# Loading each half batch of x by sixteen transfers of 112 tokens

## The chip, the cores and the metric

The program runs on one core of a Trainium2 chip. The core has a matrix engine (TensorE, PE in the profile), a vector engine (VectorE, DVE), a scalar engine (ScalarE, ACT), GpSimd (POOL) and SyncE (SP), each with an instruction queue of its own that it works off in order, and 16 DMA engines, which move data between the chip's memory and the on-chip buffer. In this kernel SyncE and ScalarE issue plain transfers and GpSimd issues the indexed ones. The metric is the device time of one execution, in microseconds (us); less is better.

## The reference

Two layers are computed one after the other. The first is a causal convolution over time with a softmax over its seven taps, with one set of taps for each of eight heads of 24 channels:

```python
x_pad = np.concatenate([np.zeros((B, pad, D), dtype=np.float32), x], axis=1)
x_unf = x_pad[:, idx, :].reshape(B, S, K, H, group)
out = np.einsum('hk,bskhg->bshg', w, x_unf)      # B, S, D = 8, 3584, 192; K = 7; H = 8
```

The second is a mixture of eight experts over the 28672 tokens that come out. Tokens and experts are paired greedily by their logits, with room for 3584 tokens in each expert, and every token then goes through the two layers of its expert:

```python
logits = x @ w_gate
...                                               # each token to one expert, 3584 per expert
h = np.maximum(x[mask] @ w1[e], 0.0)              # D = 192 -> F = 1024
out[mask] = h @ w2[e]                             # F -> D
```

## The kernel before

The tokens are cut into 16 half batches of 1792 tokens, and a half batch into 16 runs of W = 112 tokens. The convolution is a matrix product: the tile `X` of a half batch has 118 partitions (six tokens of halo and 112 of the run), 16 runs and 192 channels, and `TH[0:118, h]` is the banded matrix of head h. `conv(i)` runs the eight heads: a matmul into one of four PSUM banks named `cv`, which ScalarE copies into the tile `a`. Behind the eighth copy ScalarE issues the store of `a` into the table `attn` in memory (L209). There are two buffers `a`, so the first copy of conv(i) has to wait until the store of half batch i-2 has landed.

`load(i)` fills X by two transfers from SyncE: the halo (L194 where a batch begins, with a memset by GpSimd beside it, otherwise L197) and the 112 tokens of all 16 runs (L198). There are three X buffers. The main loop over i issues load(i+2), then conv(i), whose store follows, so a half batch adds a halo, a load and a store to the transfers, in that order in the program. load(i+2) takes the buffer of conv(i-1), and SyncE waits for the matmuls of that.

Between the heads of conv(i), the function `mid` gives out the work of the half batches before: transposes `aT` on VectorE, the split of `aT` into `hi` (ScalarE) and `lo` (GpSimd, sometimes VectorE), and the matmuls `pl` of the gate's logits for half batch i-2. The hooks add steps of the routing (threshold, counts, lists; tiles such as `X0`, `X1`, which the profile also names X, and `oa`, `bg`, `t_t`), mostly on VectorE. In which order they are given out is set when the program is built, by a model of the three compute engines' pace that leaves DMAs out of account. At i = 14 SyncE is given the first six transfers of expert weights (`raw`, L1142 to L1145), behind load 15. After the 16 half batches the experts run: gathers of rows of `attn` (GpSimd), matmuls `ph` and `y`, and indexed stores of the result.

Every transfer of SyncE and ScalarE signals its landing on one of eight semaphores. The program takes these in turn over the transfers of both engines, in the program's order, and a transfer that takes a semaphore again is issued only after the transfer eight before it, the last one on that semaphore, has landed.

Of the kernel before, what the change touches and what calls it, by code (L numbers as in the profile page):

```python
# [14 lines left out]
NE, D, NTOK, F, CAP = 8, 192, 28672, 1024, 3584  # L15
W, HW_, NHB = 112, 16, 16
# [95 lines left out]
def build(ctx, tc, nc, x, weight, wg, attn, LT, wk):  # L112
# [75 lines left out]
    def load(i):  # L188
        t = X[i] = k.xp[i % 3].tile([118, 16, D], F32, name="X")
        b, hf = divmod(i, 2)  # L190
        o = x.offset + (b * 3584 + hf * 1792) * D
        if hf == 0:
            P.memset(t[0:6, 0], 0.0)
            nc.sync.dma_start(t[0:6, 1:16], bass.AP(tensor=x.tensor, offset=o + (W - 6) * D,  # L194
                                                    ap=[[D, 6], [W * D, 15], [1, D]]))
        else:
            nc.sync.dma_start(t[0:6], bass.AP(tensor=x.tensor, offset=o - 6 * D, ap=[[D, 6], [W * D, 16], [1, D]]))  # L197
        nc.sync.dma_start(t[6:118], bass.AP(tensor=x.tensor, offset=o, ap=[[D, W], [W * D, 16], [1, D]]))  # L198

    def conv(i, mid):  # L200
        t = X.pop(i)
# [58 lines left out]
    def logits_t(i):  # L260
# [10 lines left out]
        if not last:  # L271
            V.tensor_tensor(o, o, v[:, 1], op=OP.add)

    k.load, k.conv, k.transp, k.split, k.logits, k.logits_t = load, conv, transp, split, logits, logits_t
    k.toeplitz, k.gate_ops, k.transp_last, k.logits_last = toeplitz, gate_ops, transp_last, logits_last
    return k
# [1336 lines left out]
```

## Time and profile before

| | |
|---|---|
| time, median of 3 runs | 1388.71 us (1386.31 to 1390.99) |
| the profiled execution, its time | 1390.04 us |
| its span, first to last instruction | 1388.2 us |
| mean granted TensorE clock | 0.971 of full speed |
| TensorE busy | 1303.3 us (94%) |
| VectorE busy | 1074.7 us (77%) |
| ScalarE busy | 631.2 us (45%) |
| GpSimd busy | 737.2 us (53%) |
| SyncE's DMA queue (q1) | 63888 packets, 120.75 MB |
| ScalarE's DMA queue (q10) | 28928 packets, 22.02 MB |
| loads of x (L198) | 16 transfers of 1344 KB |
| stores of `attn` (L209) | 16 transfers of 1344 KB |

The profile is of one execution. Engines are busy side by side, so the busy times add up to more than the span. Most calls of VectorE, ScalarE and TensorE pass through one helper, so their rows all bear line 53 and are told apart by their tiles. A row of the timeline has start, duration, engine, line and operation, `out<-in` by the tiles' names, and in brackets how long the engine sat idle just before and what released it. A DMA's row shows how long its issue took, not when it landed; when a transfer landed is seen where an engine waits for it, and from the rows of the DMA queues, which give packets, MB and the time that the packets took as a share of the 16 engines in a window.

### The profile page before, as it was taken

How to read it: one execution, taken by the hardware profiler on the slowest of the kernel's cores; microseconds unless marked ns; L12 is line 12 of the kernel's file. 1: busy time of each engine (PE TensorE's matmuls, PEld its weight loads, DVE VectorE, ACT ScalarE, POOL GpSimd, SP SyncE). 2: the span in 40 equal slices, each digit the busy share in tenths (PEclk: the TensorE clock that was granted, in tenths of full speed). 3: DMA queues.
4: the chain of work that ended last, by engine and by line, in shares of the span. 5: the costliest groups of instructions: out<-in, count | busy, mean ns of one | idle time of the engine just before them, and what ended most of it. 6: DMA issues, size and time to landing. Idle time of an engine off the chain costs nothing.

```text
span 1388.2 us, 21399 instructions
## 1 busy us (share of the span) xinstructions
PE 1303.3 (94%) x7459; PEld 1110.2 (80%) x7459; DVE 1074.7 (77%) x2358; ACT 631.2 (45%) x1292; POOL 737.2 (53%) x729
## 2 busy tenths in 40 slices
PE   5988898998989999999999999999999999999997
PEld 2544565887878888888888888888888888888886
DVE  7598963876988988888765778788787888878782
ACT  4745474567645555454334333333333333333331
POOL 5655466668866766666554444444443444444322
PEclk9988897999989999999999999999999999999999
DMA  9996668659771432432232251324322213141100
GB/s 230 287 263 164 171 214 283 225 193 299 261 242 54 141 134 93 139 132 84 94 122 75 96 181 44 101 84 139 99 89 90 90 49 136 43 145 40 41 29 29
DMA packets 114436, 188.28 MB, mean 136 GB/s; under 512 B 12352, under 2 KB 86544, under 8 KB 110096
## 3 DMA queue, kind: packets, MB, share of 16 engines
q1 hardware_dynamic: 63888, 120.75, 27.4%
q0 software_dynamic: 21504, 44.07, 10.1%
q10 hardware_dynamic: 28928, 22.02, 4.8%
q8 instruction: 60, 0.98, 0.3%
q14 instruction: 56, 0.46, 0.1%
HBM read 114.44 MB, written 72.35 MB: 135 GB/s over the span
## 4 chain that ended last, share of the span: by engine, by line
PE 61%; DVE 23%; ACT 6%; DMA 4%; issue 3%; POOL 2%; SPq 1%; POOLq 0%; DVEq 0%; ACTq 0%
PE ph L53 27%; PE y L53 27%; DVE X L53 5%; DVE hl L53 5%; PE bg L53 3%; DVE xs L53 2%; DMA attn<-a 2%; ACT hh L53 2%; PE cv L53 2%; DVE aT L53 2%; DVE oa L53 2%; ACT xa L53 1%; DMA raw<-in_moe_w_dram 1%; POOL xg L1206 1%; ACT hi L53 1%
## 5 line engine op out<-in xcount | busy, mean ns | idle before, releaser
L53 PE MATMUL y<-w,hh 128*128 128x384 f32 x1792 | 542.0, 357 | 0.0
L53 ACT ACTIVATE hh<-ph 128x512 fp32r<-128x512 f32 x448 | 267.3, 597 | 482.4 <-PE ph L53 324.8
L53 DVE SCALAR_TENSOR_TENSOR hl<-ph,hh 128x512 fp32r<-128x512 f32 x448 | 307.8, 687 | 212.5 <-ACT hh L53 199.2
L53 PE MATMUL y<-w,hl 128*128 128x192 f32 x1792 | 450.4, 251 | 0.0
L53 PE MATMUL ph<-xa,w 128*128 128x512 f32 x1344 | 407.2, 411 | 23.2 <-DVE hl L53 21.0
L53 PEld LDWEIGHTS y<-w,hl 128*128 128x128 f32 x1792 | 342.6, 191 | 15.6
L53 PEld LDWEIGHTS y<-w,hh 128*128 128x128 f32 x1792 | 338.2, 189 | 20.2 <-issue 3.1
L1289 POOL DMA_INDIRECT out_dram<-yo,ib x128 | 126.9, 991 | 310.4 <-DVE yo L53 299.7
L53 PEld LDWEIGHTS ph<-xa,w 128*128 128x128 f32 x1344 | 222.2, 192 | 59.2 <-DVE hl L53 33.2
L53 DVE STREAM_TRANSPOSE xs<-xg 32x128 f32<-32x128 f32 x744 | 224.6, 302 | 11.9
L53 PE MATMUL ph<-xd,w 128*128 128x512 f32 x448 | 180.2, 402 | 0.0
L53 PE MATMUL ph<-xd,dl 128*128 128x512 f32 x448 | 176.5, 394 | 0.0
L1206 POOL DMA_INDIRECT xg<-attn,ib x128 | 129.8, 1014 | 40.1 <-issue 40.1
L226 POOL TENSOR_TENSOR lo<-aT,hi 128x768 fp32r<-128x768 f32 x50 | 93.4, 1898 | 74.4 <-ACT hi L53 74.4
L1289 POOL DMA_INDIRECT out_dram<-yo,ia x96 | 104.0, 1083 | 47.3 <-POOL yo L1288 22.6
L1206 POOL DMA_INDIRECT xg<-attn,ia x96 | 113.1, 1178 | 28.8 <-issue 27.0
L53 ACT ACTIVATE yt<-y 128x192 f32<-128x192 f32 (+1 forms) x224 | 87.6, 391 | 89.6 <-PE y L53 79.3
L53 PE MATMUL cv<-X,TH 118*128 118x384 f32 x256 | 109.1, 559 | 18.5 <-DVE TH L53 12.0
L1288 POOL TENSOR_TENSOR yo<-yt 128x192 f32<-128x192 f32 x88 | 61.9, 703 | 109.4 <-ACT yt L53 108.8
L53 PEld LDWEIGHTS cv<-X,TH 118*128 118x128 f32 x256 | 50.7, 211 | 64.5 <-issue 14.2
L53 PEld LDWEIGHTS ph<-xd,w 128*128 128x128 f32 x448 | 85.7, 191 | 19.9 <-issue 0.8
L53 PEld LDWEIGHTS ph<-xd,dl 128*128 128x128 f32 x448 | 85.5, 191 | 19.9 <-POOL dl L1187 0.3
(246 smaller groups left out, 1371.0 us busy)
## 6 DMA issues: line engine op xcount, KB each, us to landing
w<-kw SPq DMA_DIRECT2D x16, 1536.0 KB
w<-kv SPq DMA_DIRECT2D x16, 1536.0 KB
X<-in_x_dram SPq DMA_DIRECT2D x16, 1344.0 KB
attn<-a ACTq DMA_DIRECT2D x16, 1344.0 KB
kw<-w SPq DMA_DIRECT2D x48, 256.0 KB
kv<-w SPq DMA_DIRECT2D x32, 384.0 KB
raw<-in_moe_w_dram SPq DMA_DIRECT2D x32, 192.0 KB
raw<-in_moe_w_dram SPq DMA_DIRECT2D x16, 256.0 KB
```

The lines of the kernel that those rows point to most:

```text
L53: return f(*a, **k)
L226: eng.tensor_tensor(lo, aT, hi.bitcast(F32), op=OP.subtract)
L1206: self.nc.gpsimd.indirect_dma_start(out=t[:, b], out_offset=None, in_=self.attn[0:rows], in_offset=bass.IndirectOffsetOnAxis(ap=idx[b], ax ...
L1288: nc.gpsimd.tensor_tensor(o, t[:, 0:D], t[:, D:2 * D], op=OP.add)
L1289: st = nc.gpsimd.indirect_dma_start(out=self.out, out_offset=bass.IndirectOffsetOnAxis(ap=idx, axis=0), in_=o, in_offset=None, bounds_chec ...
```

## The change

The transfer of the 112 tokens of all 16 runs is replaced by 16 transfers, one for each run. The same bytes go to the same places: each piece is 112 rows of 768 bytes, consecutive in memory, into 112 partitions of one run's slice of X. The halo's transfer stays as it is.

```diff
         else:
             nc.sync.dma_start(t[0:6], bass.AP(tensor=x.tensor, offset=o - 6 * D, ap=[[D, 6], [W * D, 16], [1, D]]))
-        nc.sync.dma_start(t[6:118], bass.AP(tensor=x.tensor, offset=o, ap=[[D, W], [W * D, 16], [1, D]]))
+        for w in range(16):
+            nc.sync.dma_start(t[6:118, w], bass.AP(tensor=x.tensor, offset=o + w * W * D, ap=[[D, W], [1, D]]))
```

## The prediction

> **What bounds the kernel now.** I began with the page's slices and its chain that ended last. The stage that reads x (matmuls `cv`) ends at about 203 of 1388 us; behind it TensorE is the bound and nothing loads x.
>
> ```profile
> span 1388.2 us, 21399 instructions
> PE 61%; DVE 23%; ACT 6%; DMA 4%; issue 3%; POOL 2%; SPq 1%; POOLq 0%; DVEq 0%; ACTq 0%
> ```
> ```profile
> L53 PE MATMUL cv<-X,TH x256: 483/486/1007, 12.0 to 202.6; 118*128 118x384 f32 x128
> ```
>
> Then I read the chain of waits from 0 to 130 us. Columns: start, length (us), what.
>
> ```profile
> 12.02 7.28 PE cv L53 x12
> ...
> 21.47 14.53 DMA attn<-a
> ...
> 36.09 0.87 ACT a L53 x2
> ...
> 51.62 12.11 DMA attn<-a
> ...
> 63.82 0.87 ACT a L53 x2
> ...
> 69.25 2.46 DVE lo L53
> ...
> 72.67 0.56 DVE X L53
> ```
>
> Two stores of `attn` lie on it, 26.6 us together; from about 69 us on VectorE carries it. No load of x is on it, and no row of the table of waits names x as what a matmul waited for. That table for 0 to 210 us has, for the stores (total, times, longest):
>
> ```profile
> ACT a L53 <- DMA attn<-a: 15.9, 5, 5.9
> ```
>
> ScalarE's timeline shows the five places. Store i is issued right behind the last copy of conv(i); the first copy of conv(i+1) then waits for store i-1, whose `a` buffer it takes.
>
> ```profile
> 30.19 0.31 ACTq L209 DMA_DIRECT2D attn<-a  x1
> 36.09 0.87 ACT L53 ACTIVATE a<-cv 128x384 f32<-128x384 f32 x2 [5.93 <-DMA attn<-a]
> ...
> 42.64 0.31 ACTq L209 DMA_DIRECT2D attn<-a  x1
> 44.19 0.87 ACT L53 ACTIVATE a<-cv 128x384 f32<-128x384 f32 x2 [1.58 <-DMA attn<-a]
> ...
> 51.62 0.32 ACTq L209 DMA_DIRECT2D attn<-a  x1
> 54.28 0.87 ACT L53 ACTIVATE a<-cv 128x384 f32<-128x384 f32 x2 [2.68 <-DMA attn<-a]
> ...
> 60.83 0.31 ACTq L209 DMA_DIRECT2D attn<-a  x1
> 63.82 0.87 ACT L53 ACTIVATE a<-cv 128x384 f32<-128x384 f32 x2 [3.02 <-DMA attn<-a]
> ```
>
> So store 0 (issued at 21.47) landed at 36.0, store 1 at 44.15, store 2 at 54.25, store 3 at 63.8: 14.5, 14.0, 11.6 and 12.2 us each. Why so long, the DMA rows tell (queue, packets, MB, share): q1 is SP's, q10 ScalarE's. First 62 to 66 us, behind a load issued at 59.47 and the store at 60.83; then 67 to 71; last 187 to 193, a store without any load.
>
> ```profile
> 59.47 0.38 SPq L198 DMA_DIRECT2D X<-in_x_dram  x1
> ```
> ```profile
> q1 hardware_dynamic: 1182, 0.90, 104.8%
> q10 hardware_dynamic: 54, 0.04, 3.1%
> ```
> ```profile
> q10 hardware_dynamic: 1572, 1.20, 88.7%
> q1 hardware_dynamic: 335, 0.25, 19.8%
> ```
> ```profile
> 186.96 0.31 ACTq L209 DMA_DIRECT2D attn<-a  x1
> ```
> ```profile
> q10 hardware_dynamic: 1799, 1.37, 75.6%
> ```
>
> A store issued 1.4 us behind a load hardly moves until the load is nearly through (0.04 MB beside 0.90), then runs at 0.3 MB/us. Alone it takes about 6 us (issued at 186.96, its 1.37 MB moved by 193). A load that went in ahead thus costs a store some 6 us.
>
> **The change part by part.** *Issue.* SP gives out 16 pieces of 84 KB in place of one transfer of 1344. One issue costs about what it did:
>
> ```profile
> 28.16 0.27 SPq L194 DMA_DIRECT2D X<-in_x_dram  x1
> 28.48 0.33 SPq L198 DMA_DIRECT2D X<-in_x_dram  x1
> ```
>
> 16 x 0.35 = 5.6 us of SP per load, about the 6 us that a load moves. SP waits most of the time; nothing else is in its queue there except, behind load 15, the six weight loads (`raw`), which start some 8 to 10 us later than at 171.15. Their first reader covers that:
>
> ```profile
> 171.15 1.27 SPq L1142 DMA_DIRECT2D raw<-in_moe_w_dram  x1
> ...
> 202.02 0.62 ACT L53 ACTIVATE w<-raw 128x512 fp32r<-128x512 f32 x1
> ```
>
> The cost is nothing; without that cover it would be up to those 10 us.
>
> *Order of the two queues.* A store is no longer behind 1792 rows given out at once, but behind the few pieces that went before it. That removes up to 6 us of each store's time.
>
> *New waits.* The program's eight DMA semaphores go round among SP's and ScalarE's transfers, and a transfer waits until the one eight before it has landed. Today such waits exist but are small (SP's waits, 30 to 60 us):
>
> ```profile
> SPq L197 <- DMA attn<-a: 7.2, 1, 7.2
> ...
> SPq L194 <- DMA attn<-a: 2.5, 1, 2.5
> ```
>
> They hide below SP's wait for the buffer. With 18 transfers per half batch (halo, 16 pieces, store), eight back means: piece 6 of load i+2 waits for store i-1; piece 8 for piece 0; and **store i waits for piece 8 of load i+2**, on ScalarE's in-order queue, with all copies of conv(i+1) behind it, and TensorE behind those after four banks. Pieces 6 to 15 start when store i-1 has landed, and store i when piece 8 has: a ring store, pieces 6 to 8, next store.
>
> *The ring's period.* Pieces 6 to 8: two issues (0.7 us) and the landing of a small transfer, which the trace bounds by these two:
>
> ```profile
> 0.74 4.10 DMA wb<-in_weight_dram
> ```
> ```profile
> 297.95 2.48 DMA kd<-dl
> ```
>
> The first is at the start, the second in the middle of other work, which is nearer: 0.7+2.5 = 3.2 us (up to 4.8). The store: alone 6.0; with pieces 9 to 15 and six of the next load beside it, up to 0.9 MB more. How the two queues share when both have work, 175 to 179 us shows:
>
> ```profile
> q1 hardware_dynamic: 979, 0.75, 56.8%
> q10 hardware_dynamic: 928, 0.71, 52.7%
> ```
>
> One to one, 0.366 MB/us together: (1.38+0.9)/0.366 = 6.2, and 2.3 us until the first packet and behind the last (6.0 less 1.38/0.366): 8.5. I take the middle, 7.25. Period C = 3.25+7.25 = **10.5 us** (9.2 to 13.3 by the ends).
>
> *The sum.* (a) Start. conv(0) waits for TH until 12.02, and load 0 has moved by about 9 (q1, 4 to 9 us):
>
> ```profile
> q1 hardware_dynamic: 1637, 1.24, 109.8%
> ```
>
> That is 0.25 MB/us; eight pieces of 84 KB in flight over 2.5 to 3 us carry about the same, so loads 0 to 2 land at most 2 us later, inside that cover and the wait of conv(1) for conv(0). Store 0 then shares with 0.6 MB of load 2 and 0.5 of load 3: 2.5 MB at 0.35 is 7.1 us from 22.5, landing at 30 instead of 36. Piece 8 of load 3 lands at 33.2, store 1 goes out, the first copy of conv(2) comes at 33.65 instead of 36.09: **-2.4 us** (end points of store 0: 28.5 to 31.5, so -3.9 to -0.9). (b) From there to the first copy of conv(5) the kernel before took (63.82-36.09)/3 = 9.24 us a half batch; the ring takes 10.5: 3 x 1.26 = **+3.8 us**. Under 9.24 TensorE's own need decides:
>
> ```profile
> 41.00:50.00 9.00, 9.00 (x37) 5.85 (x37) 6.82 (x11) 6.66 (x14) 5.41 (x4) 1.00 0.95 239
> ```
>
> it is busy all 9.0 us of that period, so no more than about 0.5 us a period is to be had, -1.6 in three. (c) From 72 us on VectorE sets periods of 9.3 to 24 us (one of 14 in the next row), all but those from 82 and 137 us wider than the ring; a load has two periods to land. Nothing is gained there either: no copy waits for a store any more.
>
> ```profile
> 93.00:107.00 14.00, 10.63 (x33) 6.19 (x32) 13.55 (x27) 5.72 (x13) 6.91 (x5) 0.88 0.71 203
> ```
>
> (d) conv must wait on eight semaphores instead of two: three or four more wait instructions on TensorE's queue. The trace has no duration for one there; bounds 0 and 0.1 us each. I take 0.05, so 4 x 0.05 for conv(2): **+0.2**. In conv(3) to conv(5) the ring hides it, later VectorE; uncovered in all 16 at the upper bound it would be 16 x 0.4 = 6.4.
>
> Sum -2.4+3.8+0.2 = +1.6 us. The instruction order of the engines is the same and the stages behind begin where this one ends, so the difference passes to the end. The profiled execution took 1390.04 us around its span of 1388.2, 1.3 above the median of 1388.71, within the spread of the three; so 1391.6 for such an execution and **1390.3 us** for the median. 0.3%, about what a measurement here can tell from no change, is 4.2 us.
>
> A rule of the Trainium skill speaks against the change: "DMA: Bandwidth & Descriptors", section "Rules for kernel authors", advises 1 MiB per DMA and merging many small transfers, and its fit for transfers issued by GpSimd, 2.0 us plus bytes over 436 GB/s, would by my estimate give 2.2 us for a piece, close to the 2.48 of the `kd` row. By 2.2 the period would be 10.15 and the sum some +0.5. The same page, section "Queues, rings and completion order", says that an engine takes turns between queues that have work; 175 to 179 us agrees, 62 to 66 us (0.90 to 0.04) does not. "Perfetto Trace Analysis", section "DMA Instruction — HWDGE (DVE, Sync)", says that the generator of descriptors is locked for one DMA at a time, which would explain the 62 to 66 rows; no row shows the generator.
>
> **The rivals.**
> 1. *Slower by the same ring.* Place: ScalarE, before each store, 30 to 75 us. Price 3 x (C-9.24), and some 1 us more in the period of 10.4 us at 82. It decides from C = 11.4 on (-2.4+6.5+0.2 = +4.3). For it: the 4.10 us of `wb`, which makes C 12.05 and the sum -2.4+8.4+0.2+1 = +7.2, **1396 us**. Against: that was the first transfer of all. Chance 0.29.
> 2. *Faster: the store overtakes the load, the ring stays slack.* Store 6.0, pieces 3.2: C = 9.2, TensorE decides at 8.7. Start -3.9 with store 0 at 28.5, then -1.6: -5.5, **1383.2 us**. For it: all five waits, 15.9 us, are for stores late behind loads. Against: at 28.5 store 0 must meet almost nothing of load 3. Chance 0.12.
> 3. *Nothing changes in the order*: the pieces go into the queue so quickly that a store is behind them as it is behind one load, and the eight semaphores are never short. **1388.7 us.** Against: SP needs 5.6 us to give them out and must wait for landings after eight. Chance 0.09.
> 4. *Pieces land one after another*, 16 x 2.48 = 40 us a load, where two periods give 18: conv waits some 20 us in each of 14 half batches, **about 1670 us**. That is the rule on small transfers taken at its word. Against: the six `raw` transfers, issued 0.6 to 1.3 us apart from 171.15 on, moved together beside a store (180 to 183 us):
>
> ```profile
> DMA packets 958, 1.18 MB, mean 393 GB/s; under 512 B 80, under 2 KB 563, under 8 KB 958
> ```
>
> Chance 0.01.
>
> **How the numbers follow.** The forecast as reckoned, within 0.3%, has 0.49, and rival 3 joins it: same 0.58. Slower 0.30 (rivals 1 and 4), faster 0.12. The likeliest is 1390.3 us. The range takes in rival 2's and rival 1's times with the late end of store 0 (+1.5): 1383 to 1398; about 0.08 lies on either side.
>
> **What would show it.** Right: store 0 lands by about 30 us instead of 36; SP stands for `attn<-a` in front of piece 6 of each load; ScalarE's wait in front of a store is for x; stores 1 to 4 are issued some 10.5 us apart; the first copy of conv(5) stands near 65; behind 72 us the rows are shifted alone. Wrong: first copies 8.7 us apart (rival 2), over 11.4 apart (rival 1), matmuls that wait for x (rival 4), or the start of conv(0) moved past 12 us by load 0. If the stage behind 72 us changes its length by itself, part (c) has failed.

## The result and the profile after

The changed kernel takes 1428.88 us (median of 4 runs, 1426.83 to 1430.77), the kernel before 1389.5 us in the runs beside it: a ratio of 1.0287, 95% interval 1.0267 to 1.0308, so some 40 us slower (39.4 by the medians, 40.2 by the spans of the two profiles). The forecast was 1390.3 us and its range ended at 1398. The profiled execution took 1430.17 us.

From the page of the changed kernel: the span, the chain that ended last by engine, SyncE's queue, and the group of the conv matmuls (behind the last bar: idle time before them, and what ended most of it).

```profile
span 1428.4 us, 21694 instructions
...
q1 hardware_dynamic: 67728, 120.77, 25.8%
...
PE 62%; DVE 17%; DMA 7%; ACT 6%; SPq 3%; issue 3%; POOL 2%; POOLq 0%; ACTq 0%; DVEq 0%
...
L53 PE MATMUL cv<-X,TH 118*128 118x384 f32 x256 | 109.6, 564 | 64.7 <-DMA X<-in_x_dram 37.2
```

VectorE's share of the chain fell from 23 to 17%, DMA's rose from 4 to 7%, and that of SyncE's queue (SPq) from 1 to 3%. SyncE's queue moves the same 120.8 MB. Matmuls now wait for x, 37.2 us in all; before, none did.

Where the time went is read from the issues of the stores. Store 1, store 5 and store 15 go out at 30.19, 70.37 and 206.63 us before, and here:

```profile
39.47 0.31 ACTq L210 DMA_DIRECT2D attn<-a  x1
...
102.50 0.31 ACTq L210 DMA_DIRECT2D attn<-a  x1
...
246.71 0.35 ACTq L210 DMA_DIRECT2D attn<-a  x1
```

So 9.3 us are lost up to store 1, 22.9 more up to store 5 (63.0 instead of 40.2), and 7.9 more up to store 15 (144.2 instead of 136.3). What comes after is as long as before: 1428.4-246.7 = 1181.7 against 1388.2-206.6 = 1181.6. The busy times of the stretch that lost most, first of the kernel before, then of the changed one (window, its length, PE, PEld, VectorE, ScalarE, GpSimd, granted clock, DMA share, GB/s):

```profile
30.19:70.37 40.18, 36.54 (x131) 22.62 (x130) 25.09 (x32) 26.21 (x52) 24.63 (x16) 0.98 1.03 293
```
```profile
39.47:102.50 63.03, 39.54 (x131) 25.38 (x129) 23.48 (x32) 26.99 (x52) 24.63 (x16) 0.77 0.65 184
```

The same work (131 matmuls, 52 operations of ScalarE) stands in 23 us more. TensorE is busy 3.0 us longer with it, at a granted clock of 0.77 instead of 0.98; no other compute engine is busy even 1 us longer, and the DMA engines, full before, are a third idle. So some 20 of the 23 us are waiting, not work; over the whole span TensorE is busy 1305.1 instead of 1303.3 us. Who waits, SyncE's own waits tell (0 to 250 us; total, times, longest):

```profile
SPq L199 <- DMA attn<-a: 73.8, 11, 11.4
SPq L167 <- DMA attn<-a: 10.0, 1, 10.0
```

SyncE stood 83.8 us in front of pieces of x, and of the gate's weights (L167), until a store of `attn` had landed. Its timeline shows the first such place and the one at load 5:

```profile
16.90 12.04 SPq L167 DMA_DIRECT2D wgr<-in_moe_w_gate_dram  x4
28.98 0.34 SPq L194 DMA_DIRECT2D X<-in_x_dram  x1
...
65.42 0.28 SPq L197 DMA_DIRECT2D X<-in_x_dram  x1
65.74 19.76 SPq L199 DMA_DIRECT2D X<-in_x_dram  x16
```

Load 2 goes out at 28.98 instead of 13.05 us, and the sixteen pieces of load 5 take 19.8 us to give out.

The 9.3 us up to store 1 come from the first place, but not through load 2, which conv(1) doesn't read. The gate's weights come late, and with them GpSimd's work on them, VectorE's transposes behind that, and ScalarE's split `hi`, which stands in its queue in front of the copies of conv(1). The first row is GpSimd's and the second ScalarE's, both of the changed kernel; the third is the second's counterpart before:

```profile
29.33 0.22 POOL L172 CAST GH<-wgr 32x48 fp32r<-32x48 f32 x1 [9.59 <-DMA wgr<-in_moe_w_gate_dram]
34.12 0.84 ACT L53 ACTIVATE hi<-aT 128x768 fp32r<-128x768 f32 x1 [11.93 <-DVE aT L53]
```
```profile
24.84 0.84 ACT L53 ACTIVATE hi<-aT 128x768 fp32r<-128x768 f32 x1 [2.10 <-DVE aT L53]
```

The second place, load 5, lies on the chain of waits, which follows it to the next store but one:

```profile
71.56 6.75 DMA attn<-a
...
78.33 0.31 SPq L199
...
83.86 1.65 SPq L199
...
85.60 1.34 SPq L194
...
88.08 3.25 DMA X<-in_x_dram
91.33 1.61 PE cv L53 x2
...
102.50 6.65 DMA attn<-a
```

Store 3 goes out at 71.56 and lands at 78.31. Only then SyncE gives out the other thirteen pieces of load 5, to 85.5. conv(5) has its data at 91.3, and store 5 goes out at 102.50. That is 30.9 us for two half batches, where the kernel before took 18.75 (51.62 to 70.37). TensorE's timeline has the same two half batches earlier and here:

```profile
60.16 1.62 PE L53 MATMUL cv<-X,TH 118*128 118x384 f32 x2 [11.79 <-DMA X<-in_x_dram]
91.31 1.62 PE L53 MATMUL cv<-X,TH 118*128 118x384 f32 x2 [11.71 <-DMA X<-in_x_dram]
```

**Why load 5 waits for store 3** stands in the list of transfers of the built program. The text above said that the eight semaphores are dealt out in the program's order. They are dealt out in the order of the scheduler's list, in which a store stands well ahead of the place that it has in the source. Some entries of the changed kernel (position, transfer, semaphore); the semaphore that each of these transfers names in the trace agrees:

```
 29  store 0                      5
 37  gate's weights, second       5
 51  store 1                      3
 59  load 3, piece 0              3
 75  store 2                      3
 83  load 4, piece 6              3
 90  store 3                      2
 98  load 5, piece 3              2
```

The transfer eight places behind store i is a piece of load i+2, not of load i+3 (for store 0, it is the gate's weights). With three buffers, load i+2 could run while conv(i) and conv(i+1) did. Now it can't be finished before conv(i) is, its result stored and the store landed. In the kernel before, the semaphore of store 0 came back at load 5, that of store 2 at load 7: five half batches later.

### The profile page after: what moved, and what is told of

Read it like the earlier page. It is cut to its first block, busy times and chain, and to the rows that moved or that the text cites. A ratio compares the mean times of both kernels' runs of the same rounds, so it can differ in the third digit from the quotient of the medians.

```text
span 1428.4 us, 21694 instructions
## 1 busy us (share of the span) xinstructions
PE 1305.1 (91%) x7459; PEld 1115.0 (78%) x7459; DVE 1072.0 (75%) x2358; ACT 631.6 (44%) x1292; POOL 735.8 (52%) x729
## 4 chain that ended last, share of the span: by engine, by line
PE 62%; DVE 17%; DMA 7%; ACT 6%; SPq 3%; issue 3%; POOL 2%; POOLq 0%; ACTq 0%; DVEq 0%
PE ph L53 28%; PE y L53 27%; DVE hl L53 5%; DVE X L53 4%; DMA attn<-a 4%; PE bg L53 3%; SPq L199 2%; PE cv L53 2%; DVE xs L53 2%; ACT hh L53 2%; PE pl L53 1%; DMA raw<-in_moe_w_dram 1%; ACT xa L53 1%; DMA X<-in_x_dram 1%; ACT a L53 1%
## 5 line engine op out<-in xcount | busy, mean ns | idle before, releaser
L53 PE MATMUL cv<-X,TH 118*128 118x384 f32 x256 | 109.6, 564 | 64.7 <-DMA X<-in_x_dram 37.2
L53 PEld LDWEIGHTS ph<-xd,w 128*128 128x128 f32 x448 | 85.5, 191 | 20.0 <-issue 0.8
```

What stands on the lines that cost most here:

```text
L53: return f(*a, **k)
```

## The experiments

Two theories stood against each other. **S**: the loss is the wait for a semaphore that a store holds. **R**: a piece of 84 KB costs more than its share of one transfer, in issuing or moving. Under R the loss grows with the number of pieces, 40.2 us for 15 more.

**Many transfers without pieces.** The load stays whole; fifteen small transfers go ahead of it.

```diff
+        for w in range(15):
+            nc.sync.dma_start(k.dm[i % 3][0:112, w:w + 1], bass.AP(tensor=x.tensor, offset=o + w * W * D, ap=[[D, W], [1, 1]]))
         nc.sync.dma_start(t[6:118], bass.AP(tensor=x.tensor, offset=o, ap=[[D, W], [W * D, 16], [1, D]]))
```

> One transfer per load as in the kernel before, but 15 small transfers of 112 x 4 bytes (into a tile that nothing reads) are issued just ahead of it, so that the eight semaphores go round as fast as with 16 pieces: in the program's list the semaphore of store i comes back at a small transfer of load i+2. Theory S (semaphores: a load is held until a store two half batches earlier has landed): as slow as the changed kernel, +32 to +46 us, matmuls waiting for x at every second half batch, stores of 6.5 to 7 us. Rival R (a piece of 84 KB is itself slow to issue or to move): the bytes go in one transfer, so at most +5 us for 15 more issues in a queue that mostly waits.

Measured 1473.42 us, ratio 1.0618 [1.0569, 1.0666]: 86 us slower, far over the 46 that I gave S. The first two rows are SyncE's waits (0 to 300 us), the third is TensorE's.

```profile
SPq L200 <- DMA attn<-a: 61.8, 11, 11.0
SPq L200 <- DMA X<-in_x_dram: 44.5, 15, 5.2
```
```profile
PE cv L53 <- DMA X<-in_x_dram: 85.6, 14, 15.4
```

The wait for stores is there with whole loads, 61.8 us of it. The 44.5 us are this experiment's own: here SyncE also waits for transfers eight before that read x, which in the changed kernel cost 3.4 us. And the whole load stands behind all fifteen. So a load needs no cutting to be late; the size of the loss isn't comparable.

**Fewer pieces.** Six pieces make eight transfers per half batch.

```diff
-        for w in range(16):
-            nc.sync.dma_start(t[6:118, w], ...)
+        w = 0
+        for n in (3, 3, 3, 3, 2, 2):
+            nc.sync.dma_start(t[6:118, w:w + n], ...)
+            w += n
```

> Six pieces (3, 3, 3, 3, 2, 2 runs): halo, six pieces and store are eight transfers, so from store 5 on a store's semaphore comes back at the next store and no longer at a load; before that store 1 to 4 come back at loads three half batches later. Theory S: between -6 and +4 us of the kernel before. Rival R (cost per piece, 40.2 us for 15 more pieces): 5 more pieces, +13 us.

Measured 1387.84 against 1387.79 us, ratio 1.0005 [0.9984, 1.0026]. R's 13 us would be 1.0094. SyncE waited 17.1 us in loads for stores here, four times, each time in a load three half batches behind the store. TensorE's timeline has one wait for x here behind the first conv, conv(4) for load 4, which in the list is held by store 1:

```profile
50.94 1.30 PE L53 MATMUL cv<-X,TH 118*128 118x384 f32 x2 [4.50 <-DMA X<-in_x_dram]
```

Eight and two pieces, with `range(0, 16, 2)` and `range(0, 16, 8)`:

> Eight pieces of two runs. In the program's list stores 2 to 12 come back at loads three half batches later or at the last two pieces of those, stores 0 and 1 at the last piece of the load two later. Theory S: 0 to +10 us, most of it ahead of 45 us. Rival R: 7 more pieces, +19 us.

Measured 1394.94, ratio 1.0051 [1.002, 1.0082], 7 us; R's 19 us would be 1.0137. SyncE waited for stores in eight pieces too, but mostly in loads three half batches later:

```profile
SPq L199 <- DMA attn<-a: 37.4, 9, 9.0
```

Half as much waiting, a sixth of the loss. So it isn't the length of the wait alone that costs; how far ahead of its use the held load stands is the likely reason, which the runs by place below bear out.

> Two pieces of eight runs. Stores come back at loads four half batches later, later at other stores: no wait that matters. Theory S: -4 to +2 us. Rival R: one more piece, +2.7 us.

Measured 1389.22, ratio 1.0003 [0.9979, 1.0027]. Both theories allow it.

**Sixteen pieces that no store can hold.** The stores go to GpSimd, whose transfers have other semaphores; once with one transfer per load, once with sixteen.

```diff
-        A.dma_start(attn[i * 1792:(i + 1) * 1792].rearrange("(w p) d -> p w d", p=W), a[0:W])
+        P.dma_start(attn[i * 1792:(i + 1) * 1792].rearrange("(w p) d -> p w d", p=W), a[0:W])
```

> One transfer per load as before, but the stores of attn are issued by GpSimd, whose transfers have eight semaphores of their own. A pair with the next run, which alone tells: its own time may be -5 to +15 us of the kernel before, since GpSimd also does the subtractions lo.

> Sixteen pieces per load, stores issued by GpSimd, so no load can be held by a store's semaphore any more; still at most eight pieces under way. Theory S: within 6 us of the run before it (pool_store_1). Rival R (cost per piece): 40 us slower than that run.

On this chip the kernel before took 1376.34 us. With one transfer 1389.91 (1.0085 [1.0059, 1.011]), with sixteen 1397.76 (1.0136 [1.0098, 1.0173]): 7.9 us apart by the medians, with intervals that overlap. S had allowed 6, R 40. From the six and the four runs the difference can be put between some 2 and 13 us. So the pieces by themselves cost some 8 us, a fifth of the loss, and hardly more than a third. What that is, SyncE's timeline of the run with sixteen shows, and TensorE's waits:

```profile
19.23 7.63 SPq L199 DMA_DIRECT2D X<-in_x_dram  x16
...
27.31 14.14 SPq L199 DMA_DIRECT2D X<-in_x_dram  x16
```
```profile
PE cv L53 <- DMA X<-in_x_dram: 21.9, 6, 11.3
```

Sixteen pieces take 7.6 us to give out, and 10.1 to 14.1 for most loads with a store beside them, so some loads land late even so: behind the first conv, matmuls wait 10.6 us for x.

**Where in the loop.** Sixteen pieces for some loads only, one transfer for the others.

```diff
+        if 2 <= i < 7:        # i >= 7 and i < 2 in the other two
         for w in range(16):
             nc.sync.dma_start(t[6:118, w], ...)
+        else:
+            nc.sync.dma_start(t[6:118], ...)
```

> Sixteen pieces for loads 2 to 6 alone; stores 0 to 4 come back at loads 2 to 6. Theory S: conv(1) to conv(6) is where the periods are short, so most of the loss is here: +15 to +30 us. Rival R: 5 of 16 loads, 40.2 x 5/16 = +12.6 us.

> Sixteen pieces for loads 7 to 15 alone; stores 5 to 13 come back at loads 7 to 15. Theory S: VectorE's long periods hide most of the wait there, as the two traces show (136.3 against 144.2 us from store 5 to store 15): +3 to +12 us. Rival R: 9 of 16 loads, +22.6 us.

> Sixteen pieces for loads 0 and 1 alone. The semaphore of store 0 comes back at the second of the four transfers of the gate's weights, ahead of load 2 in SP's queue. Theory S: load 2 goes out only when store 0 has landed at about 28 us, instead of at 13, and GpSimd's work on the gate starts late; with loads 2 to 6 (+1.7%) and 7 to 15 (+0.4%) known, what is left of +2.9% is +0.7%, so +5 to +12 us. Rival R: 2 of 16 loads, +5 us, with load 2 issued at about 17 us.

Loads 2 to 6: ratio 1.0173 [1.0135, 1.0211] from two runs, +24 us. Loads 7 to 15: 1.0041 [1.0017, 1.0065], +6 to +8 us, though SyncE waited longer there:

```profile
SPq L200 <- DMA attn<-a: 50.0, 10, 11.7
```
```profile
SPq L200 <- DMA attn<-a: 27.5, 3, 11.3
```

The first row is of loads 7 to 15, the second of loads 2 to 6. Five loads lose three times or more what nine lose; R would have it the other way round. The nine lose nearly all of it in one place. By the semaphores in that trace stores 7 to 13 come back at loads 9 to 15, as expected (stores 5 and 6 only at loads 8 and 9). Yet from store 5 to store 14 the stage takes 126.7 us, where the kernel before took 125.7; from store 14 to store 15 it takes 16.4 instead of 10.6. There conv(15) begins at 200.94 instead of 194.81 us, because load 15 was held by store 13:

```profile
200.94 1.62 PE L53 MATMUL cv<-X,TH 118*128 118x384 f32 x2 [5.38 <-DMA X<-in_x_dram]
```

Loads 0 and 1: 1.0028 [1.0003, 1.0052], 4 us by the ratio and 6 by the medians, at the low end of the 5 to 12 that I gave S. R's 5 fits as well, so the time doesn't tell the two apart; the trace does. SyncE stood 10.0 us at the gate's weights, and store 1 went out at 39.29 us, 9.1 late, as in the changed kernel. By store 15 (212.15 instead of 206.63, on another chip than the trace before) only 5.5 us of that were left. The three parts add up to 2.4% of the 2.9%.

**Versions that might be faster.** The trace before shows stores of 11.5 to 14.5 us behind a load. First: loads from load 3 on, halo and body, issued by ScalarE, behind the store.

```diff
     def load(i):
+        eng = A if i > 2 else nc.sync
...
-        nc.sync.dma_start(t[6:118], ...)
+        eng.dma_start(t[6:118], ...)
```

> One transfer per load as before, but from load 3 on issued by ScalarE right behind the store of the half batch before, so that the store's rows go into the DMA engines first. If the order of the two is what made stores of 12 to 14 us, they fall to 6 to 8 us, the five waits for a store (15.9 us) go, and the time falls by 2 to 7 us. If the sum of what both move is the bound up to 70 us, it stays within 2 us.

Measured 1383.12 against 1374.29 us, ratio 1.0056 [1.0031, 1.0081]: slower. ScalarE's timeline:

```profile
21.39 0.36 ACTq L210 DMA_DIRECT2D attn<-a  x1
21.84 5.01 ACTq L198 DMA_DIRECT2D X<-in_x_dram  x1
26.89 1.66 ACTq L199 DMA_DIRECT2D X<-in_x_dram  x1
28.60 0.87 ACT L53 ACTIVATE a<-cv 128x384 f32<-128x384 f32 x2 [7.25 <-DMA raw<-in_moe_w_dram]
```

No copy waits for a store any more, but the halo behind the store holds ScalarE's queue for 5.01 us here and 2.15 to 3.5 us at the next five places, and the copies with it. The 7.25 us of idle time in the last row are these three issues (21.39 to 28.55); the transfer named in its brackets is only the last event that the profile could put there. The version changes one thing more, which wasn't tried by itself: SyncE has no load left to wait at, so it gives out the expert weights from 18.67 us on instead of 171.15, four of them just ahead of this store and halo.

```profile
18.67 0.35 SPq L1143 DMA_DIRECT2D raw<-in_moe_w_dram  x1
```

Then six pieces in the first loads only, in loads 2 and 3, and in loads 0 to 3 with two pieces for the others:

> Six pieces for loads 2 and 3 alone, one transfer for the others. Store 0 comes back at store 1, store 1 at load 4, the others at loads five half batches later. The run with six pieces everywhere was 3.7 us ahead at store 3 and lost it where conv(4) waited for load 4. Theory S: load 4 is still held by store 1, but goes out whole at once then; -4 to +2 us. If the lead came from the pieces of loads 4 and 5 too, 0.

> Six pieces for loads 0 to 3, two for the others; store 1 comes back at load 4, stores 2 and 3 at loads four later, stores 5 to 10 at stores. Theory S: -4 to +2 us, as the run before.

Ratios 0.999 [0.9967, 1.0012] and 0.9994 [0.9967, 1.0021]: no change. Both were ahead at store 3 (48.75 and 49.22 instead of 51.62 us) and lost most of it by store 5 (69.56 and 70.52 instead of 70.37). No version was found that beats the kernel before.

## Why the prediction was wrong

*What bounds the kernel* held, and with it the reason to look at stores rather than loads.

*The order of the two queues* held. Stores take 6.6 to 8.1 us up to store 5, where they took 11.5 to 14.5; I had taken 7.25, and the store that I read as 6.0 alone landed after 6.7. No copy waits for a store any more; the 15.9 us are gone.

*New waits: this step failed.* It said that piece 6 of load i+2 waits for store i-1 and store i for piece 8 of load i+2, from eight transfers back in the order of the source. The list that deals the semaphores has another order: a piece of load i+2 waits for **store i**. The two rows of SyncE's waits that I quoted would have shown it, had I counted: store 0 came back at the halo of load 5, seven places back in the source, not eight.

*The ring's period* failed with it. The ring I reckoned runs store, pieces, store and has no conv in it, 10.5 us a half batch. The true one runs store i, the rest of load i+2, conv(i+2), store i+2: 6.75 us, 7.2 us to give out thirteen pieces, 5.8 until the last has landed beside store 4, and 11.2 of conv(5), 30.9 us for two. That is 15.5 a half batch and gives the 22.9 us of the middle stretch, which (b) put at +3.8.

*Part (a)*, -2.4 us by store 1, turned into +9.3: store 0 landed at 27.63, earlier than the 30 reckoned, but it holds the gate's weights, and ScalarE's copies of conv(1) stand behind work that needs these. The sum had no term for the gate's weights. Load 2, behind them, was 16 us late instead of at most 2. *Part (c)*, nothing beyond 72 us, came out at +7.9. Of this, 5.7 us arise between stores 14 and 15 (16.3 instead of 10.6), where conv(15) waits for load 15 and that for store 13; up to store 14, VectorE's longer periods cover the ring of 31 us for two half batches but for 2.2 us. *The issue* of a piece was 0.35 us, measured 0.46 and more (7.42 us for the sixteen of load 0). That is hidden at the start, where conv(0) began at 11.47 instead of 12.02, and may be part of the 8 us of the pair with GpSimd's stores. The cover of the weight loads behind load 15 held, barely: they go out at 230.76 and the chain of waits has the last of them landed at 242.5, just ahead of their first reader at 242.57. *Part (d)*, the waits on more semaphores, wasn't tried by itself. The prediction found no duration for one on TensorE's queue, but the trace has them: 176 instead of 129, the shortest 0.051 us, so the 0.05 was fair, and 47 more make 2.4 us if none is hidden.

Of the rivals, the first named the semaphores and the right sign, but a place (ScalarE in front of a store) where nothing waited, and a price of 7 us. The fourth expected matmuls to wait for x, but because pieces land one after another. They don't: the sixteen of load 0 were there when conv(0) began at 11.47 us. The rule of the Trainium skill on small transfers ("DMA: Bandwidth & Descriptors", section "Rules for kernel authors") points the right way here, yet the runs give what it is about, the cost of the pieces themselves, some 8 of the 40 us, and none with six pieces of 168 to 252 KB. What the Trainium skill says in "Perfetto Trace Analysis", section "DMA Instruction — HWDGE (DVE, Sync)", of a generator locked for one DMA at a time agrees with the rows of ScalarE above (5.01 us for an issue behind four weight loads and a store, 2.15 to 2.7 where a store alone had just gone out); no row shows the generator itself.

## What to carry to other kernels

Where transfers share a few semaphores in turn, the number of transfers per loop pass decides which earlier transfer each one waits for; count it in the built program's list, not in the source. A prefetch is only as deep as the latest result that it waits for: one wait on a store of this pass turned two half batches of lead into none. Before cutting a transfer, choose the number so that the semaphore of a store comes back at a store, as with six pieces here from store 5 on; that avoids the loss, and gained nothing over one transfer.

## What the runs showed of the hardware

Issuing a transfer isn't a fixed cost. Behind a store of 1344 KB that has just gone out, an issue takes longer, on the same queue and from another engine. On ScalarE's queue the halo of 72 KB, 0.27 us by itself, takes 2.15 to 2.7 us behind stores 2 to 5 (5.01 behind store 0, where weight loads had gone out too). On SyncE behind store 4, issued at 82.70, a piece takes 1.65 us instead of 0.43, and a halo 1.34 instead of 0.28.
